# Attention loaded and computed by pairs of heads, and the first gate weights converted in two halves

## Chip, cores, metric

One core of one Trainium2 chip. The metric is the device time of one execution in microseconds (us); medians of the runs in the fast state are quoted (the record marks each run as fast or slow). The profiled span is about 2 us shorter than the time (850.6 against 852.7 in the profiled run of the kernel before).

## The reference, cut to what matters

```python
# batch 8, heads 8, seq 576, head_dim 64; fp32.  w1, w2, w3, w_out arrive as 64-bit floats.
kv  = einsum('bhsd,bhse->bhde', k, v)
out = einsum('bhsd,bhde->bhse', q, kv)
x   = out / sqrt(mean(out*out, -1) + 1e-6) * g_norm      # then (B,H,S,D) -> (B*S, H*D)
h   = ((x @ w1) * (x @ w2)) @ w3
return h @ w_out                                         # d_model 512, d_ff 1024
```

## The kernel before

A sequence of 576 is 4 x 128 positions and 64 left over. The left rows of q wait and are done for two batches at a time (in the odd batches); those of k and v enter kv as a fifth step. Batch 0 comes first, for without its x no gate can start. Its gates are plain matmuls that run while ScalarE (ACT) and VectorE (DVE) convert the 64-bit weights. In the "fold" stage that follows, w3 @ w_out is multiplied out and batch 1's attention is put between the matmuls. From then on every stage is a Winograd product of one batch (helper at line 432: matrices cut in quarters, seven products of quarters in place of eight) with eight pieces of the next batch's attention between its matmuls. The order on TensorE is the order of the program; in batch 0 that holds for ACT, DVE and the DMA queue too.

```python
ps_mm = ...(bufs=5, PSUM)      # one bank each; TensorE writes its results into banks
ps_at = ...(bufs=3, PSUM)      # the attention's banks

# attention(b): half = four heads, i = first or second 128 columns of q
def kv(half):                  # 20 matmuls, then copies into the block-diagonal kv_bd
    ...                        #   2 copies on DVE, 2 on ACT, each 64 x (2 x 64)
def q_t(i, half):              # 4 transposes into one bank, ACT copies it to qT
    ...
def product(i, half):          # 4 matmuls qT x kv_bd into one bank, then norm
    ...
def norm(o_ps, dst):
    nc.scalar.activation(sq[:, cols], o_ps[:, cols], AF.Square)                  # ACT
    nc.vector.tensor_reduce(out=inv, in_=sq..., axis=AX.X, op=ALU.add)           # DVE
    nc.scalar.activation(inv, inv, AF.Sqrt, scale=1.0 / D, bias=eps_col)         # ACT
    nc.vector.reciprocal(inv, inv)                                               # DVE
    nc.vector.tensor_tensor(out=dst, in0=o_ps..., in1=inv..., op=ALU.mult)       # DVE
def turn(i, half):             # 4 transposes, ACT copies them to xT, times g
    ...

# one later batch: eight pieces between the matmuls of the stage
for half in range(2):
    pieces += [[(kv, half), (q_t, 0, half)], [(product, 0, half), (q_t, 1, half)],
               [(product, 1, half), (turn, 0, half)], [(turn, 1, half)]]
if b % 2:
    pieces[5] += [(q_t_left,)]; pieces[6] += [(product_left,)]; pieces[7] += [(turn_left,)]

def convert(dst, raw):         # 64-bit to fp32: 2 passes on ACT (L142, L143), then 4 on DVE
    ...                        #   (L144, L147, L150, L154)

# batch 0
load_half(0, 0, inp); load_half(0, 1, early_pool)      # k, kl, v, vl, q of four heads each
...
keep_warm(16)                                          # matmuls on the identity, result unused
for name in ("kv0", "q_t00", "q_t10", "product00", "product10"): first[name]()
keep_warm(4)
for name in ("kv1", "q_t01", "q_t11", "turn00", "product01", "turn10", "product11"): first[name]()
keep_warm(4)
for name in ("turn01", "turn11"): first[name]()
...
for _ in range(2): convert_next("w")
for f in range(KF):
    convert_next(...)                                  # two blocks ahead of the gates
    gate(0, f)                                         # 8 matmuls of 128x512, L379
```

## Time and profile before

852.41 us median of 4 runs (851.16 to 852.93). Stages of the profiled run, by the start of the first matmul of each:

| stage | from | length | what TensorE does |
|---|---|---|---|
| batch 0 attention | 0 | 32.72 | idle for 13.0 us |
| gates of batch 0 | 32.72 | 57.83 | busy; half clock until 38.38 |
| fold, attention of batch 1 | 90.55 | 75.73 | busy |
| output product of batch 0 | 166.28 | 24.18 | busy |
| batches 1 to 7 and the left rows | 190.46 | 660.14 | busy, but for the last outputs |

### The profile page before, as it was taken

The numbers are of one execution on the slowest core, as the hardware profiler recorded it, in microseconds if no ns is written. First come the engines' busy times: TensorE is split into PE (matmuls) and PEld (weight loads), VectorE is DVE, ScalarE is ACT, GpSimd is POOL, SyncE is SP. The second block draws the span as 40 slices with busy tenths as digits, with TensorE's granted clock in tenths as the row PEclk, the third lists the DMA queues.
The fourth block names the chain that finished last, engine by engine and source line by source line (L and its number), as shares of the span: only waits on it lengthen the run. The fifth ranks groups of instructions, "written<-read, shape, count | busy, mean of one in ns | idle before, by whom it ended". The sixth has DMA issues, their size and how long they took to land.

```text
span 850.6 us, 10819 instructions
## 1 busy us (share of the span) xinstructions
PE 831.8 (98%) x4480; PEld 683.8 (80%) x4480; DVE 378.3 (44%) x718; ACT 249.2 (29%) x447; POOL 0.7 (0%) x6
## 2 busy tenths in 40 slices
PE   7599999999999999999999999999999999999997
PEld 7244556588888888888888888888888888888886
DVE  3698963393460356035503550355045503433330
ACT  3555532213331333133313331332133312212220
POOL 0000000000000000000000000000000000000000
PEclk9699999999999999999999999999999999999999
DMA  9669803003101221032013210310120000001002
GB/s 282 215 213 318 273 23 93 1 25 106 57 25 44 88 58 37 25 106 57 25 50 81 57 37 27 105 57 25 50 81 1 2 34 17 1 0 50 1 1 49
DMA packets 52112, 59.41 MB, mean 70 GB/s; under 512 B 14688, under 2 KB 47456, under 8 KB 51040
## 3 DMA queue, kind: packets, MB, share of 16 engines
q1 hardware_dynamic: 52064, 58.73, 21.9%
q8 instruction: 35, 0.57, 0.3%
q14 instruction: 13, 0.11, 0.0%
HBM read 49.28 MB, written 9.44 MB: 69 GB/s over the span
## 4 chain that ended last, share of the span: by engine, by line
PE 96%; DVE 1%; ACT 1%; DMA 1%; issue 0%; SPq 0%; ACTq 0%; DVEq 0%
PE mm L432 71%; PE mm L379 7%; PE mm L419 6%; PE at L295 3%; PE at L232 3%; PE at L254 2%; PE at L327 2%; PE at L312 1%; PE mm L406 1%; DMA v_sb<-in_v_dram 1%; DVE inv L274 0%; DVE xn L282 0%; PE at L264 0%; PE at L336 0%; ACT sq L272 0%
## 5 line engine op out<-in xcount | busy, mean ns | idle before, releaser
L432 PE MATMUL mm<-xT,w_sb 128*128 128x256 f32 x672 | 154.2, 379 | 0.0
L432 PEld LDWEIGHTS mm<-xT,w_sb 128*128 128x128 f32 x672 | 127.7, 190 | 17.4
L432 PE MATMUL mm<-xc,ws 128*128 128x256 f32 x512 | 115.7, 379 | 0.0
L432 PEld LDWEIGHTS mm<-xc,ws 128*128 128x128 f32 x512 | 97.3, 190 | 13.2
L445 ACT COPY u<-mm 128x512 f32<-128x512 f32 x82 | 48.1, 586 | 193.8 <-PE mm L432 193.8
L432 PE MATMUL mm<-w3o_sb,ab 128*128 128x256 f32 x432 | 96.2, 379 | 0.0
L432 PEld LDWEIGHTS mm<-w3o_sb,ab 128*128 128x128 f32 x432 | 82.1, 190 | 11.6 <-issue 0.5
L445 ACT COPY p<-mm 128x512 f32<-128x512 f32 x82 | 48.1, 586 | 139.2 <-PE mm L432 139.2
L379 PE MATMUL mm<-xT,w_sb 128*128 128x512 f32 x128 | 58.0, 617 | 6.6 <-DVE w_sb L154 6.6
L432 PE MATMUL mm<-os,as 128*128 128x256 f32 x288 | 63.6, 379 | 0.0
L432 PEld LDWEIGHTS mm<-os,as 128*128 128x128 f32 x288 | 54.7, 190 | 7.4
L432 PE MATMUL mm<-xc,w_sb 128*128 128x256 f32 x256 | 60.5, 379 | 0.0
L379 PEld LDWEIGHTS mm<-xT,w_sb 128*128 128x128 f32 x128 | 25.3, 199 | 38.9 <-issue 31.3
L419 PE MATMUL mm<-wo_sb,w3T 128*128 128x512 f32 x128 | 56.4, 593 | 0.0
L274 DVE TENSOR_REDUCE inv<-sq 128x8 f32<-128x512 f32 (+1 forms) x40 | 25.1, 628 | 69.5 <-ACT sq L272 69.4
L545 DVE TENSOR_TENSOR c<-mm,u 128x512 f32<-128x512 f32 x32 | 22.0, 688 | 73.9 <-PE mm L432 73.9
L432 PE MATMUL mm<-xT,ws 128*128 128x256 f32 x224 | 53.3, 381 | 0.0
L247 DVE COPY kv_bd<-at 64x128 f32<-64x128 f32 x32 | 9.2, 287 | 95.8 <-PE at L232 95.5
L432 PEld LDWEIGHTS mm<-xc,w_sb 128*128 128x128 f32 x256 | 46.8, 190 | 5.4
L419 PEld LDWEIGHTS mm<-wo_sb,w3T 128*128 128x128 f32 x128 | 23.7, 190 | 26.9 <-issue 26.8
L578 DVE TENSOR_TENSOR o_sb<-mm,u 128x512 f32<-128x512 f32 x9 | 6.2, 691 | 86.4 <-issue 74.0
L432 PEld LDWEIGHTS mm<-xT,ws 128*128 128x128 f32 x224 | 40.7, 190 | 4.7
(87 smaller groups left out, 920.8 us busy)
## 6 DMA issues: line engine op xcount, KB each, us to landing
k_sb<-in_k_dram SPq DMA_DIRECT2D x16, 512.0 KB, 4.3
v_sb<-in_v_dram SPq DMA_DIRECT2D x16, 512.0 KB, 5.4
q_sb<-in_q_dram SPq DMA_DIRECT2D x16, 512.0 KB, 4.0
raw<-in_moe_w_dram SPq DMA_DIRECT2D x16, 512.0 KB, 5.8
raw<-in_moe_w_dram SPq DMA_DIRECT2D x8, 1024.0 KB, 5.1
out_dram<-o_sb SPq DMA_DIRECT2D x16, 512.0 KB, 2.6
raw<-in_moe_w_out_dram SPq DMA_DIRECT2D x4, 1024.0 KB, 5.1
kl_sb<-in_k_dram SPq DMA_DIRECT2D x16, 64.0 KB, 4.4
```

The lines of the kernel that those rows point to most:

```text
L232: nc.tensor.matmul(kv_ps[e * D:(e + 1) * D, r, :], lhsT=k_sb[:, h, cols] if j < J else kl_sb[:, h, :], rhs=v_sb[:, h, cols] if j < J else ...
L247: nc.vector.tensor_copy(out=to[:, :, e, :], in_=kv_ps[e * D:(e + 1) * D])
L254: nc.tensor.transpose(qt_ps[:, h, :], q_sb[:, h, i * P:(i + 1) * P], ident)
L274: nc.vector.tensor_reduce(out=inv, in_=sq[:, cols].rearrange("p (h d) -> p h d", d=D), axis=AX.X, op=ALU.add,)
L295: nc.tensor.matmul(o_ps[:, h * P:(h + 1) * P], lhsT=qT[i, half][:, h, :], rhs=bd[:, half * HB + h, :], start=True, stop=True,)
L312: nc.tensor.matmul(o_ps[l * L:(l + 1) * L, r * D:(r + 1) * D], lhsT=st["qT"][rows, r, l * L:(l + 1) * L], rhs=kv_bd[l][rows, 2 * r + e, rows],
L327: nc.tensor.transpose(t_ps[:, r, j, :], st[i, half][:, j, 2 * r:2 * r + 2, :], ident)
L379: nc.tensor.matmul(g_ps, lhsT=w_sb[:, f, w, c, :], rhs=xT[T][:, c // 2, :, c % 2, :], start=(c == 0), stop=(c == NP - 1),)
L419: nc.tensor.matmul(f_ps, lhsT=t[:, j, :], rhs=wo_sb[:, j, :], start=(j == 0), stop=(j == KF - 1))
L432: nc.tensor.matmul(ps[:, u, :], lhsT=lhsT(a_name, u, c), rhs=rhs(b_name, c),  start=(u == 0 and c == 0 and to is None), stop=(c == chunks ...
L445: nc.scalar.copy(t, ps)
L545: nc.vector.tensor_add(c, one, two)
```

## The change

Intent: smaller first loads, so that attention starts sooner; batch 0 as a pipeline of four pairs; and half of the first weight block converted before the last transposes, so that the gates need not wait for a whole block. The later batches go by pairs too.

```diff
-    def load_half(b, half, pool):            # k, kl, v, vl, q of four heads
+    def load_pair(b, r, pool):               # k, v, q of two heads
+    def load_kv_left(b):                     # kl, vl of all eight heads
-        def kv(half):
+        def kv(r):                           # 10 matmuls, 4 copies of 64x64
-        def q_t(i, half):
+        def q_t(r):                          # both halves of q's columns, two heads
-            pieces += [ ... as above ... ]
+        pieces = [
+            [(begin, 0)],                    # begin(r): kv(r), q_t(r), next loads
+            [(product, 0), (begin, 1)],
+            [(turn, 0), (product, 1)],
+            [(begin, 2), (turn, 1)],
+            [(product, 2), (begin, 3)],
+            [(turn, 2), (product, 3)],
+            [(turn, 3)],
+            [],
+        ]
         if b % 2:
-            pieces[5] += [(q_t_left,)]
+            pieces[4].append((q_t_left,))
 ...
+        keep_warm(10)
+        for r in range(NP):
+            kv(r)
+            q_t(r)
+            if r:
+                turn(r - 1)
+            keep_warm(2)
+            product(r)
+        block_0 = convert_next("w", 2)       # a generator: two halves
+        next(block_0)
         keep_warm(4)
-        for name in ("turn01", "turn11"):
-            first[name]()
+        turn(NP - 1)
+        all_of(block_0)
```

(Cut: the buffers, qT from four to three of them, the bodies that follow from the new grouping, and the places of the later loads.)

## The prediction

> **What bounds the kernel now.** I read the page first (busy shares, slices, clock), then the waits of TensorE, then a table of windows cut where the waits ended, then the chain of the first 36 us in order of time, last the timeline of TensorE in one later batch.
>
> From the page:
>
> ```profile
> PE   7599999999999999999999999999999999999997
> PEclk9699999999999999999999999999999999999999
> ```
>
> ```profile
> PE mm L379 <- DVE w_sb L154: 6.6, 1, 6.6
> ```
>
> TensorE is busy in every slice but the first two and the last, and its clock is low only in slice 2. The second fence is from the list of TensorE's waits: the largest is one wait of 6.6 us, of the first gate matmul for the first converted block of weights.
>
> The table of windows (start:end, length, then busy time per engine, granted clock, DMA share, GB/s):
>
> ```profile
> 0.00:32.72 32.72, 19.70 (x192) 17.20 (x193) 12.97 (x24) 14.57 (x27) 0.70 (x6) 0.88 0.82 239
> 32.72:39.00 6.28, 6.28 (x8) 2.71 (x9) 6.14 (x8) 2.21 (x2) 0.00 (x0) 0.55 0.87 301
> 166.40:673.90 507.50, 507.50 (x2994) 447.34 (x2993) 218.14 (x464) 143.84 (x286) 0.00 (x0) 1.00 0.16 51
> ```
>
> Before 32.72 us TensorE is idle for 13 us. From there to the end it is never idle but for the last outputs' 5.7 us. So only two things can be won: the date of the first gate (32.72) and the half clock after it. The clock by half microseconds is 0.5 from 24.77 to 38.38, so the first 5.66 us of gates ran at half rate and lost 2.83 us. Anything that adds TensorE time after 32.72 is paid in full.
>
> What sets 32.72, from the chain in order of time (start, us, what):
>
> ```profile
> 9.31 0.28 DVE kv_bd L247
> 9.63 0.30 DVE kv_bd L247
> ...
> 10.02 0.26 ACT kv_bd L245
> 10.29 0.26 ACT kv_bd L245
> ...
> 10.57 0.59 ACT qT L256
> ...
> 11.21 1.17 PE at L295 x8
> ...
> 12.40 0.61 ACT sq L272
> ...
> 13.03 0.70 DVE inv L274
> ...
> 13.76 0.31 ACT inv L280
> ...
> 14.09 0.22 DVE inv L281
> ...
> 14.40 0.69 DVE xn L282
> ...
> 31.44 1.24 DVE w_sb L154
> ...
> 32.72 3.78 PE mm L379 x4
> ```
>
> This is latency and not throughput: a hand from TensorE to DVE, to ACT, to TensorE and back. From the end of kv at 9.29 to the end of the first normalisation at 15.09 it is 5.80 us. The second product of a half follows only 1.96 us later (17.05), because its norm overlaps the first one's and the kv copies are shared. The second half ends at 24.91. The fixed tail comes then: two turns, two ACT passes over 1024 columns, four DVE passes, to 32.72, which is 7.81 us.
>
> **What the Trainium skill says.** "VectorE: DVE Perf Modes", section "The TRN2 errata", gives an fp32 tensor_tensor as (N+151)/0.96 ns and says that small tiles pay the fixed part each. The trace agrees: 692 ns for 512 columns (691 by the formula), 422 for 256 (424), and the 128-column kv copy 287 (291). Halving the kv copies thus saves 64 columns each, not half. "TensorE: Matmul & The Clock Gate", section "What's actually happening", tells of a free-running window of 3.4 us, with half clock after an idle window and full after a busy one. The trace agrees: low from 24.77 to 38.38 is 13.61 us, 3.99 windows; the window 31.6 to 35.0, busy for 2.3 of 3.4 us, did not raise it. The same page, "Part 4: PE-mode transpose", says that transposes don't count as busy in the same way; the window before the drop (21.36 to 24.77) holds 0.87 us of plain matmuls and 0.63 of transposes, which is in line with it but no proof.
>
> **The change part by part.**
>
> (a) Smaller first loads. Now kv needs 1.18 MB of k, kl, v, vl, and waits for v until 7.31. Afterwards k, v, q of one pair and all of kl, vl come first, 1.05 MB; the fifth step (kl, vl) waits last. By the bytes per half microsecond the old run had moved 1.25 MB (1.05 plus some of the next load) at about 6.7 to 6.9. The four first steps are done by then, 0.3 us are left: kv of pair 0 ends at about 7.2 against 9.29. That is a gain of 2.1 us.
>
> (b) One pair at a time. The order of instructions of the changed kernel shows ACT and DVE in strict program order: kv copies of pair r+1 come after the last norm step of pair r on DVE, ACT's kv copies wait for DVE's, and the qT copy follows on ACT. So nothing of one pair's attention overlaps the norm of the one before. One pair costs, from the chain above with 64-column copies (DVE (64+151)/0.96 = 0.22; ACT 0.26 less 64 x 0.84 ns = 0.21, the slope from 586 ns at 512 and 372 at 256 columns): DVE copies 0.02+0.47, ACT copies 0.09+0.42, qT 0.02+0.59, product 0.05+1.17, square 0.02+0.61, reduce 0.02+0.70, root 0.03+0.31, reciprocal 0.02+0.22, scaling 0.09+0.69 = 5.54 us. Turn and the two warming matmuls fit beside it (done 1.3 us after the norm, product starts at 1.67). Four pairs: 22.2 us, from 7.2 to 29.4. Before: 9.29 to 24.91, 15.6 us. A loss of 6.5 us. The pipeline that the change means to make is not there; it has four serial rounds where two rounds of two overlapped products were.
>
> (c) First weights in halves. ACT converts half a block after the last root, while DVE does the last reciprocal and scaling: it is done at about 29.5. DVE then does four passes over 512 columns, half of the 3.82 us that four took over 1024 (28.85 to 32.67) plus 0.1 for fixed parts, 2.0 us. The last turn and its copy (about 31.1) lie beside this. Gate at 29.4+2.2 = 31.6. The tail is 2.2 us in place of 7.81, a gain of 5.6. The second half is ready some 2.8 us after the gate starts and the first four matmuls take 3.5; block 1 about 6.9 after, needed at 6.97: just in time.
>
> Sum of (a) to (c): 32.72 - 2.1 + 6.5 - 5.6 = 31.5, about 31.6.
>
> (d) Clock. In a round of 5.5 us TensorE has 1.2 us idle after q_t and 0.4 before the product, and between them turn and 0.5 us of warming. A window there holds 1.85 us of work of 3.41, most of it transposes; the one that dropped held 1.5. So I expect a drop or two inside the rounds: product 1.17 becomes about 2, and so on, 0 to 3 us, taken as 1.2. Before the gate, from 1.65 us ahead of the end of the norm to 2.2 after it, only the turn runs: I put 60% on a drop there, which costs 1.7 to 3.1 us of slow gates; mean 1.4 against 2.83 now.
>
> (e) Later batches. The same matmuls, but kv in four groups a batch, not two. In the timeline a group of winograd matmuls lasts 3.55 us when kv follows and 3.46 when another follows, and q_t after kv takes 0.50 against 0.44 after a product: 0.15 us per extra group, 2 x 7 = 14 groups, up to 2.1 us on a full TensorE, taken as 1.2 since some follow a product. Sixteen more small copies a batch on DVE and ACT lie beside matmuls (DVE busy 43% in that window). Loads are issued at least two pieces ahead (12 us) and land in 4 to 6: hidden. The shorter pieces leave the norm at least 5.2 us of matmuls to hide in; I expect no new wait above 0.5 us in total.
>
> **Sum.** 852.08 + (31.6 - 32.72) + 1.2 + (1.4 - 2.83) + 1.2 = 851.9. Loads and weights that come a little quicker than I assume pull it down, so I say 851.5.
>
> **Rivals.** One: the rounds overlap well, so that a pair costs about 4 us as each product did before (15.6/4 = 3.9). For it speaks that PSUM has three banks and that kv and q_t run ahead on TensorE; against it DVE's order, which holds the next pair's kv copy behind the norm. The gate would start at 7.2 + 17 + 2.2 = 26 and with a warm clock the time would be about 843 to 846. Two: the clock drops early and stays down through the rounds (about 7 us each): gate at 37, gates still cold: 857 to 858. Three: the gates outrun the conversions. DVE needs 3.84 x 1.5 + 0.69 = 6.45 us a block on average, TensorE 6.9: close, but DVE stays ahead; if weights landed late it would cost 1 to 3 us. Before, the slow first gates gave that slack for nothing. Four: a late load for batch 1 behind weight loads on the one queue; in the fold stage each load has some 20 us, so I give it 5%, with 1 to 4 us.
>
> **Range and chances.** The start of the gates is uncertain by 1.5 us either way, the clock by 2, the extra groups by 1: together about 3 us. Range 847.5 to 855. Two per cent is 17 us; even a gate at 20 us would not reach that, and no rival reaches 869. So 98% within.
>
> **What would show it.** Right: the chain of the changed kernel repeats a round of about 5.5 us (copies DVE, copies ACT, qT, product, square, reduce, root, reciprocal, scaling) four times; kv of pair 0 ends near 7.2; the last scaling ends near 29.4; the first gate starts at 31 to 33.5; from there TensorE has no long wait and the span after the first gate is within 3 us of the 817.9 of now. Wrong: rounds near 4 us and a gate before 28 (step b), a clock of 1.0 all through or at 0.5 from 13 us on (step d), a wait for w_sb after the first gate (c), or waits of TensorE for kv_bd, xn or a load after 166 us (e).

## The result, and the profile after

857.56 us median of 4 runs (857.18 to 858.26). All outputs are right. The ratio to the kernel before is 1.0064 (95% interval 1.0046 to 1.0081). Such ratios are the mean time of one kernel's fast runs over that of the other's in the same rounds, so not quite the ratio of the medians. The change made the kernel some 5 us slower; the range of the prediction (847.5 to 855) does not hold it.

The busy row and the clock row of the page, which look better than before at first sight:

```profile
PE   7799999999999999999999999999999999999997
PEclk9999999999999999999999999999999999999999
```

Slice 2 is no longer at half clock for most of its length. But the windows by stage, cut as in the table above (start:end, length, busy time per engine, clock, DMA share, GB/s), first before and then after:

```profile
32.72:90.55 57.83, 57.83 (x128) 25.46 (x129) 50.51 (x58) 31.54 (x33) 0.00 (x0) 0.95 0.77 260
90.55:166.28 75.73, 75.73 (x377) 43.53 (x376) 41.92 (x64) 27.51 (x45) 0.00 (x0) 1.00 0.32 96
190.46:850.60 660.14, 654.39 (x3673) 576.31 (x3671) 248.98 (x521) 173.27 (x339) 0.00 (x0) 1.00 0.14 44
```

```profile
34.18:90.91 56.73, 56.73 (x128) 25.00 (x129) 52.62 (x62) 34.14 (x36) 0.00 (x0) 0.97 0.81 268
90.91:168.22 77.31, 76.11 (x378) 43.35 (x377) 42.33 (x68) 28.37 (x49) 0.00 (x0) 1.00 0.31 95
192.39:855.90 663.51, 655.72 (x3673) 575.46 (x3671) 249.02 (x545) 176.94 (x363) 0.00 (x0) 1.00 0.14 43
```

So the 5.3 us between the spans are: gates start 1.46 later, gates 1.10 shorter (the clock was low for 3.41 us of them and not for 5.66), fold 1.58 longer, later batches 3.37 longer. Most of the loss stands where the change meant nothing to happen: in stages in which TensorE was full.

The list of TensorE's waits (line <- releaser: us in total, times, longest) after 90 us, where the kernel before has none:

```profile
PE at L272 <- ACT qT L264: 2.7, 4, 0.7
PE mm L436 <- ACT low L143: 0.5, 1, 0.5
```

L272 are the transposes of q's left part, once in each odd batch. The timeline of TensorE in batch 1 shows one of the four (start, us, engine, line), after the change and then before:

```profile
133.30 0.65 PE L262 MATMUL at<-ident,q_sb 128*128 128x128 f32 x4
134.63 0.66 PE L272 MATMUL at<-ident,ql_sb 128*128 128x128 f32 x4 [0.68 <-ACT qT L264]
```

```profile
139.68 0.60 PE L254 MATMUL at<-ident,q_sb 128*128 128x128 f32 x4
140.12 0.60 PE L264 MATMUL at<-ident,ql_sb 128*128 128x128 f32 x4
```

From q_t to the left part it is 1.33 us, before it was 0.44. The piece now takes four attention banks in a row (product, kv, q_t, left part) and there are three.

In batch 0 the round of one pair is as foreseen. This is the third one (of pair 2), from the chain in order of time (start, us, what):

```profile
20.93 0.12 DVE kv_bd L254
21.08 0.24 DVE kv_bd L254
...
21.34 0.20 ACT kv_bd L252
21.56 0.21 ACT kv_bd L252
...
21.79 0.59 ACT qT L264
...
22.43 1.17 PE at L305 x8
...
23.68 0.61 ACT sq L280
...
24.31 0.70 DVE inv L282
...
25.68 0.69 DVE xn L290
```

The copies of the next pair start at 20.93, where the scaling of the pair before ends, and nothing overlaps: scalings end at 15.49, 20.93, 26.37 and 31.80. But the first round starts late. kv of pair 0 waited for the left rows of v (L240, 1.7 us) and ended at 9.06.

### The profile page after: what moved, and what is told of

Same layout as the page of the kernel before. It is cut to its first block, busy times and chain, and to the rows that moved or that the text cites. A ratio compares the mean times of both kernels' runs of the same rounds, so it can differ in the third digit from the quotient of the medians.

```text
span 855.9 us, 10920 instructions
## 1 busy us (share of the span) xinstructions
PE 834.9 (98%) x4476; PEld 684.1 (80%) x4476; DVE 379.8 (44%) x754; ACT 255.4 (30%) x481; POOL 0.7 (0%) x6
## 4 chain that ended last, share of the span: by engine, by line
PE 95%; ACT 1%; DMA 1%; DVE 1%; SPq 0%; issue 0%; ACTq 0%; DVEq 0%
PE mm L449 71%; PE mm L396 7%; PE mm L436 6%; PE at L305 3%; PE at L240 3%; PE at L262 2%; PE at L335 1%; PE mm L423 1%; PE at L322 1%; DMA q_sb<-in_q_dram 1%; DMA raw<-in_moe_w_dram 1%; ACT qT L264 0%; SPq L89 0%; PE at L272 0%; DVE inv L282 0%
## 5 line engine op out<-in xcount | busy, mean ns | idle before, releaser
L436 PEld LDWEIGHTS mm<-wo_sb,w3T 128*128 128x128 f32 x128 | 23.7, 190 | 27.6 <-issue 26.8
L563 DVE TENSOR_TENSOR ab<-c 128x256 f32<-128x256 f32 x96 | 40.6, 423 | 2.8
```

Of the source, the lines that this page charges most:

```text
L436: nc.tensor.matmul(f_ps, lhsT=t[:, j, :], rhs=wo_sb[:, j, :], start=(j == 0), stop=(j == KF - 1))
L563: nc.vector.tensor_mul(dst, c[:, 0, :], c[:, 1, :])
```

## The experiments

Ten kernels ran in three sittings, each beside the kernel before on the same chip (its medians there: 851.88, 852.25, 852.67). My main theory after the result: most of the loss is in the later batches, by a wait for a PSUM bank and by the extra kv groups; batch 0's four serial rounds eat what the halves of weights win. The rival: batch 0 and its small loads make the loss.

### 1 and 2: pairs in batch 0 only, and in the later batches only

```diff
 # e_pairs_first: the changed kernel, but attention(b) for b >= 1
-    pieces by pairs
+    pieces by halves, as in the kernel before (q_t_left in piece 5); loads stay in pairs
 # e_pairs_later: the changed kernel, but for batch 0
-    rounds of pairs, block 0 in halves
+    batch 0 by halves and block 0 whole, in the order of before; loads stay in pairs
```

> Batch 0 as in the changed kernel (pairs, first weights in halves), batches 1 to 7 computed by halves of four heads as before, loads by pairs everywhere. Theory 1 (nearly all of the loss lies after the first gate, in the later batches: 1.58 us in the fold stage and 3.37 after it, by the two traces): gate at about 34.2 as in the changed kernel, then the before's stages, 852.6 us, within 1 us of before. Rival (the loss is the serial rounds of batch 0 and loads in small pieces): stays near 857.

> The counterpart: batch 0 by halves and the first weights whole as before, batches 1 to 7 by pairs as in the changed kernel, loads by pairs everywhere. Theory 1: first gate at 32.7 to 34, the fold stage 1.6 us and the seven later stages 3.4 us longer than before, no new wait but the four of the transposes of q's left part (0.7 us each); 857 to 858.5 us. Rival: 852.5 to 854.

Measured: pairs in batch 0 only, 853.2 us (ratio 1.0021, 1.0005 to 1.0038); pairs in later batches only, 858.65 (1.0077, 1.0062 to 1.0092). The stage of the later batches of the two, in this order:

```profile
190.65:850.80 660.15, 654.39 (x3673) 576.32 (x3671) 248.98 (x521) 173.30 (x339) 0.00 (x0) 1.00 0.14 44
```

```profile
192.77:856.30 663.53, 655.71 (x3673) 575.46 (x3671) 249.07 (x545) 176.93 (x363) 0.00 (x0) 1.00 0.14 43
```

660.15 is the 660.14 of before and 663.53 the 663.51 of after; the fold stages were 75.73 and 77.32 likewise. So the 4.95 us come and go with the pairs in the later batches, and loading by pairs costs nothing there. The rival falls. Both times lie a little above what was expected (within 1 us of before, and 858.5 at most). In batch 0 the first kernel started its gates at 34.00 and the second at 33.37, where before had 32.72: with loads by pairs even the old order of work starts later.

### 3 and 4: the weights in halves, alone and undone

```diff
 # e_halves: the kernel before, one part of the change
+        block_0 = convert_steps("w", 2)
+        next(block_0)
         keep_warm(4)
         for name in ("turn01", "turn11"):
             first[name]()
+        for _ in block_0:
+            pass
 # e_whole: the changed kernel without it
-        block_0 = convert_next("w", 2)
-        next(block_0)
         keep_warm(4)
         turn(NP - 1)
-        all_of(block_0)
+        all_of(convert_next("w"))            # whole, after the last turn
```

> The kernel before with one part of the change alone: the first block of weights converted in two halves, the first ahead of the last two turns. Last scaling stays at 24.9, then the four half-width DVE passes, 2.3 us as in the changed kernel: first gate at 27.3 in place of 32.7. The clock drops near 25 as before and comes back after a busy window, so the gates lose 2 to 3.4 us to it as before: 847 us, faster than both kernels. Rival (the conversions then starve the second and third block and the gain is given back as a wait for w_sb in the gates): 850 to 852, with a wait of TensorE for w_sb of 3 us or more after the first gate.

> The changed kernel with the first block of weights converted whole and after the last turn, as before. The last scaling stays at 31.8 and the tail grows from 2.4 to 7.5 to 7.8 us: first gate at about 39.4, total 862 to 863.5. If the halves hid nothing (the last turn or the weights' arrival set the gate anyway) it stays at 857 to 858.

Measured: halves alone 846.62 us (ratio 0.9936, 0.9921 to 0.9951), undone 863.83 (1.0137, 1.0122 to 1.0152), just above its expected range. The gates started at 27.63 and 39.85. The chain of the first, just ahead of its gates:

```profile
24.77 0.56 ACT w_sb L143
...
25.36 0.44 DVE w_sb L144
25.82 0.43 DVE w_sb L147
26.25 0.61 DVE low L150
...
26.88 0.70 DVE w_sb L154
...
27.63 8.40 PE mm L387 x15
```

This part of the change wins about 5 us by itself and works in both kernels. Its own list of waits shows none for w_sb after the first gate, so the conversions keep up with gates that start 5 us earlier.

### 5: q's left part one piece later; 9: a fourth attention bank

```diff
 # e_left_later
-            pieces[4].append((q_t_left,))
+            pieces[5].append((q_t_left,))
 # e_four_banks
-    ps_mm = ...(bufs=5), ps_at = ...(bufs=3)
+    ps_mm = ...(bufs=4), ps_at = ...(bufs=4)
```

> The changed kernel with one edit: in the odd batches the transposes of q's left part move one piece later, to where no q_t of a pair stands right before them. Theory (they wait because all three attention banks are taken by the product, kv and q_t of the same piece, until ACT has copied q_t): the four waits of 0.7 us go, 2.5 to 3.4 us less than the changed kernel, 854.2 to 855; what stays above before is the extra kv groups, some 2 us. Rival (the wait is only the place where ACT's queue is seen, and comes back at the new place): 857 to 858.

> The changed kernel with four PSUM banks for attention and four for the other matmuls, not three and five; the order of instructions is left alone. Theory (the transposes of q's left part wait for a bank): the four waits of 0.7 us are gone, and with them 2 to 3 us: 854.5 to 855.5, unless four banks make the other matmuls wait, which the list of TensorE's waits would show. Rival (the wait is for ACT's queue itself, not for a bank): the four waits stay, 857 to 858.

Measured: 854.08 us (ratio 1.0022, 1.0005 to 1.0039) and 854.98 (1.0029, 1.0014 to 1.0044), against 1.0064 for the change. Both lists of waits lost all four entries of the left part. With the fourth bank nothing else in the order moved, and in batch 1 the left part followed q_t (134.39) by 0.49 us:

```profile
134.88 0.60 PE L272 MATMUL at<-ident,ql_sb 128*128 128x128 f32 x4
```

It was the bank. The fold and the later stages of e_left_later:

```profile
89.55:165.96 76.41, 75.88 (x377) 43.38 (x376) 42.34 (x68) 28.19 (x49) 0.00 (x0) 1.00 0.30 96
190.13:851.00 660.87, 655.07 (x3673) 575.49 (x3671) 249.05 (x545) 176.63 (x363) 0.00 (x0) 1.00 0.14 44
```

So the waits had cost 0.90 us in the fold (77.31 to 76.41) and 2.64 in the later batches (663.51 to 660.87), 3.54 in all. With the fourth bank it is 0.96 and 2.69. This is more than the 2.7 listed as idle, because at each of the four places the distance from q_t to the left part had grown by 0.89 us (0.44 to 1.33), of which the list counts 0.68.

What then stays above the kernel before is 0.68 us in the fold and 0.73 after it. The 0.68 stands at one place, the wait listed after ACT's L143: from the first q_t to the first block of the fold it is 1.18 us (92.27 to 93.45 in e_left_later), before it was 0.50 (94.14 to 94.64). The first kv piece is half as long as before, and the block most likely waits for the copy of its transposed w3 on DVE: the list of e_left_small names that copy for the same wait. The 0.73 is a loss less a small gain. The gate stages of the even batches are 0.30 us longer (59.23 to 59.53, two extra kv groups), those of the odd ones 0.08 shorter (62.15 to 62.07); why the odd ones don't lose is not shown.

### 6: the left rows of pair 0 alone first

```diff
-        load_pair(0, 0, inp); load_kv_left(0); load_pair(0, 1, inp)
+        # k, v of pair 0; kl, vl of its two heads; q of pair 0; pair 1; kl, vl of the other six heads
```

> The changed kernel, but only the two heads of pair 0 of the left rows of k and v are loaded first, ahead of q, and the other six heads after pair 1. Theory (kv of pair 0 ended at 9.06 and not at 7.2 because the 256-byte pieces of all heads' left rows stood before it and slowed the transfers to some 200 GB/s): kv of pair 0 ends at 7.0 to 7.6; the product of pair 0 then waits for q, near 9.7 in place of 10.7; first gate near 33, 856 to 857 us. Rival (the first load's latency sets it, not those pieces): kv stays near 9, no gain.

Measured: 856.89 us (ratio 1.0051); kv of pair 0 ended at 7.4, its product started at 9.02, the gates at 32.48. The end of kv is where the prediction had put it (7.2), and the left rows were what held it. The DMA view of the first 9 us of the kernel before and of the changed one shows what goes with it:

```profile
DMA packets 2430, 2.01 MB, mean 224 GB/s; under 512 B 592, under 2 KB 2430, under 8 KB 2430
```

```profile
DMA packets 2579, 1.72 MB, mean 191 GB/s; under 512 B 1158, under 2 KB 2579, under 8 KB 2579
```

The left rows travel in packets of 256 bytes, and the change puts those of all eight heads ahead of all loads but pair 0's: twice as many small packets, and fewer bytes in the same time, with the DMA engines equally busy (78.7% before, 79.2% after). No run separates the size of these packets from their place in the queue. The Trainium skill ("DMA: Bandwidth & Descriptors", section "Why small descriptors are slow (HBM only)") gives a 256-byte descriptor 27% of overhead; the trace agrees in direction. The gain in time was small (0.7 us, with intervals that overlap, so not clear of noise). The gates started 1.70 us earlier, but in this profiled run the clock dropped from 24.2 to 27.6 and again from 31.0 to 37.9, so that 5.4 us of the gates ran at half clock and not 3.41: a loss of 1.0 more.

### 7: the next pair ahead of this pair's norm

```diff
+        kv(0)
+        q_t(0)
+        keep_warm(2)
         for r in range(NP):
-            kv(r)
-            q_t(r)
-            if r:
-                turn(r - 1)
-            keep_warm(2)
-            product(r)
+            if r + 1 < NP:
+                kv(r + 1)
+                q_t(r + 1)
+            product(r)
+            if r:
+                turn(r - 1)
+            keep_warm(2)
```

> The changed kernel with kv and q_t of the next pair put before the product and the norm of this pair, in the order of all engines. Theory (a round is 5.4 us because the next pair's kv copies and qT copy stand in DVE's and ACT's order behind this pair's norm): rounds fall to 4.0 to 4.5 us, last scaling at 28.3 to 29.2 in place of 31.8, first gate at 30.6 to 31.6, total 854 to 855.5. Rival (the three PSUM banks or the product's latency hold the round): rounds stay above 5 us, 857.

Measured: 852.87 us (ratio 0.9997). In the chain the roots (ACT's Sqrt in the norm, L288) start at 14.71, 18.77, 22.80 and 24.92, so rounds of 4.06, 4.03 and 2.12 us in place of 5.44, and the gates at 29.23. The last round is shorter than I had said because no further pair stands before it. So the order of instructions made the serial rounds, and not banks or the latency of the product. The edit moves the order of all engines; that it was DVE's and ACT's, as step (b) of the prediction has it, is read from the chain of the changed kernel, in which DVE's copies follow the scaling at once. Three of its four runs took 852.8 to 853.1 at a mean clock of 0.994 to 0.995, one took 849.91 at 0.999: runs of one kernel differ by 3 us with the clock.

### 8: halves of weights in the kernel before, and a warm clock

```diff
         next(block_0)
-        keep_warm(4)
-        for name in ("turn01", "turn11"):
-            first[name]()
+        keep_warm(5)
+        first["turn01"]()
+        keep_warm(4)
+        first["turn11"]()
+        keep_warm(5)
```

> The kernel before with the first weights in halves (846.6 us), and with 14 warming matmuls in place of 4 around the last two turns, so that TensorE is not left idle for long before the gates. Theory (the 3.4 us at half clock after the first gate cost 1.7 us): the clock stays at 1.0 and 1 to 1.7 us go, 845 to 845.6, gate still at 27.6. Rival (the warming matmuls push the last turn back, or the gates then wait for the second block's conversion): 846.6 or more, with a wait for w_sb after the first gate.

Measured: 844.67 us (844.57 to 844.81; ratio 0.9909, 0.9892 to 0.9925), the best of all, and the steadiest. Windows of its batch 0 and its gates:

```profile
0.00:27.56 27.56, 21.86 (x212) 19.62 (x212) 11.32 (x23) 12.53 (x26) 0.70 (x6) 1.00 0.97 281
27.56:82.60 55.04, 55.04 (x128) 24.38 (x129) 52.54 (x62) 34.13 (x36) 0.00 (x0) 1.00 0.81 274
```

The clock is 1.00 throughout and the gates take 55.04 us. That squares with the others: 57.83 less half of 5.66 is 55.0, and 56.73 less half of 3.41 is 55.0. The warming matmuls fill time in which TensorE was idle and did not move the gates (27.56 against 27.63).

### 10: the pairs mended

```diff
 # e_mended: the edits of 5, 6 and 7, and
         turn(NP - 1)
+        keep_warm(6)
         all_of(block_0)
```

> The changed kernel with the three mends that were tried alone: next pair's kv and q_t ahead of this pair's norm, the left rows of pair 0 alone first, q's left part one piece later; and six more warming matmuls after the last turn. If the parts add up: first gate near 28.3, no slow gates, later stages 1.5 us longer than the kernel before's: 847 to 849.5 us, so better than before and still behind the 844.7 of the halves with warming. If they do not add up (the rounds stay bound by something else): 850 to 853.

Measured: 848.92 us (846.08 to 849.57; ratio 0.9949, 0.9928 to 0.9969). The median fell in the expected range (the profiled run, 849.57, just above it), but not by the expected way: the gates started at 31.29 and not at 28.3. Two mends clash. With the next pair's kv put ahead on TensorE, the product of pair 0 stands behind kv of pair 1, which waits first for its v and then for its left rows, which the other mend had moved behind the other loads:

```profile
PE at L248 <- DMA v_sb<-in_v_dram: 2.0, 1, 2.0
PE at L248 <- DMA vl_sb<-in_v_dram: 1.8, 1, 1.8
```

The rest came as expected: the gates ran at full clock from the start (55.04 us), and the stages after them were 1.2 us longer than in the kernel before. The 3 us of later gates fit because the range reached 2.5 us above its lower end.

## Why the prediction was wrong

It was wrong in the size and in the sign: 851.5 said, 857.56 measured. Step by step, with its own letters:

**(e) Later batches: the step that failed.** It said "I expect no new wait above 0.5 us in total" and took 1.2 us for the whole step; the two traces show 4.95. The wait for the fourth bank is 3.54 of it (experiments 5 and 9), and the wait at the head of the fold 0.68 more. Neither is among the waits (for kv_bd, xn or a load) that the prediction named as signs of a wrong step (e). I had the list of pieces and the number of banks in front of me, but looked only for the distance of a norm to its turn (5.2 us), and not for how many banks one piece takes in a row. The extra kv groups themselves cost 0.15 us each in the even batches, as the prediction had counted, and nothing on balance in the odd ones: 0.73 us after the fold, within what I had said. The Trainium skill ("Perfetto Trace Analysis", section "Optimizing Tensor Performance") says that independent matmul groups should rotate through different PSUM banks, so that copying one out overlaps the next; the trace agrees, with 0.44 us from group to group where a bank was free and 1.33 where none was.

**(a) First loads: mis-sized.** kv of pair 0 ended at 9.06, not at 7.2. I put the end at 1.25 MB moved, by the old rate. By the half-microsecond windows of the changed kernel 1.26 MB had indeed moved at 7.0 us, but the left rows of v landed only at about 8.65, when some 1.6 MB had: more of the next loads had got through before them than I counted, and between 7.0 and 8.0 at 147 to 166 GB/s. Experiment 6, which keeps the left rows of the six heads that pair 0 doesn't need out of the way, ends kv at 7.4. This is 1.9 us.

**(b) One pair at a time: right.** Rounds of 5.44 us for 5.54 said, four in series, by the order on DVE (experiment 7). With the first round mostly at half clock (6.43 us) the four took 22.7 us; I had 22.2 and 1.2 for the clock.

**(c) Halves: right, a little too cheap.** The tail was 2.38 us for 2.2 said. Experiments 3 and 4 show that this part wins 5 to 6 us. The narrow DVE passes took 0.43 us, where half of the wide ones' 0.69 would be 0.34. The (N+151)/0.96 of the page that I had cited, with the two elements a cycle that the same page ("VectorE: DVE Perf Modes", section "The perf-mode tier table") gives for an fp32 tensor_scalar in SBUF, makes an estimate of 0.42 for 512 columns and 0.69 for 1024, and the trace agrees (0.43 and 0.69). So I had the means to say 2.3.

**(d) Clock: right in kind.** One drop inside the rounds (10.3 to 13.7 us) and one at the gates, which lost half of 3.41, so 1.7 us, for 1.4 said.

Together: 1.9 for (a), 0.2 for (c), 0.3 for the clock at the gates and 3.7 for (e), less 0.7 in the rounds, make 5.4 us; with 851.9 from the prediction's sum this is 857.3.

Of the rivals, the first (rounds near 4 us) is what a better order gives and not what the change gives; the second (clock down through the rounds) and third (gates outrun the conversions) did not come, and that the second had named 857 to 858, the time that was measured, is chance; the fourth (a late load for batch 1) did not either. The one that came, a missing bank, was not on the list. What stays open is why the odd batches don't pay for their extra groups.

## What to carry to other kernels

When one engine is full, read a change first for what it makes that engine wait for, in every stage it touches: count the buffers that one piece takes in a row, not only the distance between a write and its reader. A pipeline needs the order of instructions on every engine to interleave its rounds; smaller pieces in the same order only make more serial rounds. Try the parts of a change alone: here one part was worth 5 us, and it was hidden under 5 us of loss from the rest.

## What the Trainium skill lacked or had wrong

- "TensorE: Matmul & The Clock Gate" gives the window (3.4 us, borne out: low for 3.41 us in the gates after the change, 13.6 or four windows before) but not how busy a window must be. Here a window busy for 2.3 of 3.4 us did not raise the clock, and one busy for 1.5 of 3.4 us, 0.6 of it transposes, let it drop.
- "DMA: Bandwidth & Descriptors" tells of the overhead of small descriptors, but not of what a few of them do to the loads beside them: with 1158 packets under 512 bytes of 2579 in the first 9 us the core moved 191 GB/s, with 592 of 2430 it moved 224. The order of the loads differed too, so this is a hint and no measure.
- No page that I read gives a figure for going from matmuls of 128 rows and columns to groups of 64 and back ("TensorEngine Tiling (Array Packing)" speaks of a drain, without one): the group ahead lasts 3.55 in place of 3.46 us and the transposes behind 0.50 in place of 0.44; two more such groups lengthened an even batch by 0.30 us.
